# Block-sorted attention feeding a max-of-two MLP: filler matmuls and a new order in the first batch item, and a decaying backlog for choosing the PSUM eviction engine

## The chip, the cores and the metric

The kernel runs on one core of one Trainium2 chip. A core has a matrix engine (TensorE, "PE" in the profile; its weight loads are listed apart as "PEld"), a vector engine (DVE), a scalar engine (ACT), GpSimd (POOL) and a queue engine (SP), each with its own instruction stream. They run side by side and wait for each other on semaphores. TensorE writes its results to PSUM, and only DVE and ACT read them from there here. The metric is device time in microseconds of one execution. Before the change the median of 8 runs was 173.48 us (172.91 to 175.41).

## The reference

```python
# q, k, v: (4, 8, 768, 64); sort_net: (4, 8, 8, 8)
P = sort_net
for _ in range(5):                       # softmax over rows, then columns normalised
    P = np.exp(P - P.max(-1)); P = P / P.sum(-1); P = P / P.sum(-2)
k_sorted = einsum('bhij,bhjcd->bhicd', P, k_b)      # 8 blocks of 96 keys, mixed
v_sorted = einsum('bhij,bhjcd->bhicd', P, v_b)
attn = softmax(scale * q_b @ k_sorted.T)            # inside one block of 96
x = (attn @ v_sorted) -> (3072, 512)
out = np.maximum(x @ w1, x @ w2) @ w_out            # w1, w2: 512x1024, w_out: 1024x512
```

(Shortened: small constants and keepdims are left out.)

## The kernel before

**Algebra.** The kernel uses max(a, b) = relu(a - b) + b. `w_difference` overwrites w1 by w1 - w2 in four column pieces, `moe_h` computes relu(x (w1 - w2)) into a tile `g`, and the part x w2 w_out goes through a product wc = w2 w_out. For it w2 is transposed on TensorE (`w2_transposes`) and multiplied by w_out (`w_product`). `moe_out` sums g w_out and x wc in one PSUM tile.

**Stages of one batch item.** `sort_k` and `sort_v` (or `sort_v_pair` for two items at once) mix the key and value blocks with block-diagonal matrices. `scores(b, u)` computes one of 8 pieces of the scores (four blocks, two heads), and ACT writes its exponential into an `e` tile. `values(b, u)` multiplies `e` with the values; DVE then takes a reciprocal of the row sums (`rs`) and scales the result into `x`. Two pieces of `x` make one `x_transposes` unit (pieces 0 and 1 make unit 0, and so on up to 6 and 7 for unit 3). For item 0 the transposes are done by TensorE with an eviction to `xT`; for later items SP issues DMA transposes. `moe_h(b, ch, t)` reads half of the 768 tokens (`ch`) and a quarter of w1 (`t`).

**Order.** The order is written out by hand and every engine runs its stream in order. Up to line 720 it is a prologue: five Sinkhorn rounds during which TensorE multiplies zeros (`keep_streaming`, line 75), then item 0's sorting, its first scores and values, the first two `moe_h` of item 0, and the transposes of w2. `moe_h_products(0, 0, t, (0, 2))` starts a product with half of its terms as soon as `x_transposes(0, 0)` is evicted; `moe_h(0, 0, t, "A", (1, 3))` adds the rest after `x_transposes(0, 1)`. Then a loop over the four items walks through `units` (8 `moe_h`, for item 0 4 `w_product`, 12 half `moe_out`), puts pieces of the next item's sorting and attention (`steps`) between them in proportion to a `cost` per unit, and `tail` steps at given units. `tail[2]` and `tail[3]` hold what is left of item 0: values 6, x transposes 2, values 7, x transposes 3.

**PSUM.** There are four PSUM buffers of 128 x 1024 floats (line 62), handed out again in the order in which the program releases them. A new TensorE tile therefore waits until the eviction of an older one is done.

**Choice of the eviction engine.** `evac` (line 98) copies a PSUM tile to SBUF on ACT or DVE. Some calls name the engine ("A", "D"); the others, and `moe_h` of later items, call `pick` (line 92). It keeps a sum of estimated nanoseconds per engine in `load` and takes the engine whose sum would be smaller afterwards. The sums grow over the whole kernel and are never reduced.

Of the kernel before, what the change touches and what calls it, by code (L numbers as in the profile page):

```python
# [16 lines left out]
def kernel(  # L17
# [21 lines left out]
    B, H, S, D = q.shape  # L39
# [26 lines left out]
    def ps_f32(name):  # L66
        return psum.tile([128, 1024], FP32, tag="ps", name=name)

    def ps_bf16(name):
        return psum.tile([128, 2048], BF16, tag="ps", name=name)  # L70
# [17 lines left out]


    load = {"A": 0.0, "D": 0.0}  # L90

    def pick(a_ns, d_ns):
        if load["A"] + a_ns <= load["D"] + d_ns:
            load["A"] += a_ns
            return "A"
        load["D"] += d_ns
        return "D"

    def evac(out_ap, in_ap, n, two_x=False, eng=None):
        a_ns, d_ns = (200 + n) / 1.2, (130 + (n / 2 if two_x else n)) / 0.96  # L100
        if eng:
            load[eng] += a_ns if eng == "A" else d_ns
        if (eng or pick(a_ns, d_ns)) == "A":
            nc.scalar.copy(out=out_ap, in_=in_ap)  # L104
        else:
            nc.vector.tensor_copy(out=out_ap, in_=in_ap)  # L106
# [81 lines left out]
    def w_difference(t, eng=None):  # L188
        n = DFF // 4
        (eng or nc.vector).tensor_tensor(  # L190
            out=w1_sb[:, :, t * n : (t + 1) * n],
            in0=w1_sb[:, :, t * n : (t + 1) * n],
            in1=w2_sb[:, :, t * n : (t + 1) * n],
            op=ALU.subtract,
        )
        if not eng:
            load["D"] += 600
# [313 lines left out]
    def x_transposes(b, t, eng=None):  # L511

        ih, hh = divmod(t, 2)
        x = x_tiles.pop((b, ih, hh))
        if b:
            nc.sync.dma_start_transpose(
                out=xT[:, b % 2, ih, hh].rearrange("p h (i c) -> p (h i) c", c=BLK),
                in_=x.rearrange("p t i n d -> p (t i n d)"),
            )
            return  # L520
        ps = ps_bf16("tx_ps")
        for m in range(8):
            h2, ii = divmod(m, 4)
            nc.tensor.matmul(
                ps[:, m * BLK : (m + 1) * BLK],
                x[:, h2, ii].rearrange("p n d -> p (n d)"),
                ident[0:BLK, 0:BLK],
                is_transpose=True,
                start=True,
                stop=True,  # L530
            )

        evac(
            xT[:, b % 2, ih, hh].rearrange("p h f -> p (h f)"),
            ps[:, 0 : 2 * TCH],
            2 * TCH,
            two_x=True,
            eng=eng,
        )
# [5 lines left out]
    def w2_transposes(t, eng):  # L545
        ps = ps_bf16("tw_ps")
        for n in range(16):
            fb, dmt = t * 4 + n // 4, n % 4
            nc.tensor.matmul(  # L549
                ps[:, n * 128 : (n + 1) * 128],  # L550
                w2_sb[:, dmt, fb * 128 : (fb + 1) * 128],
                ident,
                is_transpose=True,
                start=True,
                stop=True,
            )
        return lambda: evac(
            w2T[:, t * 4 : t * 4 + 4, :].rearrange("p f d -> p (f d)"),
            ps,
            2048,  # L560
            two_x=True,
            eng=eng,
        )
# [23 lines left out]
    def moe_h_products(b, ch, t, hps, n=0):  # L587
        if hps[0] == 0:
            h_ps[t] = ps_f32("h_ps")
            keep_streaming(h_ps[t], n)  # L590
        for m in range(2):
            fb = t * 2 + m
            for hp in hps:
                nc.tensor.matmul(  # L594
                    h_ps[t][:, m * 512 : m * 512 + TCH],
                    w1_sb[:, hp, fb * 128 : (fb + 1) * 128],
                    xT[:, b % 2, ch, hp % 2, hp // 2, :],
                    start=(hp == 0),
                    stop=(hp == 3),
                )  # L600

    def moe_h(b, ch, t, eng=None, hps=(0, 2, 1, 3), n=0):
        moe_h_products(b, ch, t, hps, n)
        ps = h_ps[t]
        g = gpool.tile([128, 2, TCH], BF16, tag="g", name="g")
        src = ps.rearrange("p (t f) -> p t f", t=2)[:, :, 0:TCH]
        if (eng or pick((200 + 2 * TCH) / 1.2, (130 + 2 * TCH) / 0.96)) == "A":
            nc.scalar.activation(out=g, in_=src, func=AF.Relu)  # L608
        else:
            nc.vector.tensor_scalar(  # L610
                out=g, in0=src, scalar1=0.0, scalar2=None, op0=ALU.max
            )
        g_tiles[b, ch, t] = g
# [48 lines left out]
    def att(b):  # L662

        SC = [lambda u=u: scores(b, u) for u in range(8)]
        VA = [lambda u=u: values(b, u) for u in range(8)]
        TR = [lambda t=t: x_transposes(b, t) for t in range(4)]
        return SC, VA, TR
# [17 lines left out]
    SC, VA, TR = att(0)  # L685
# [4 lines left out]
    sort_v(0, 1, 0, "A")  # L690
    q_transposes(0, 0, "D")
    sort_v(0, 2, 0, "A")
    SC[0]()
    sort_v(0, 3, 0, "D")
    SC[1]()
    q_transposes(0, 1, "D")
    VA[0]()
    SC[2]()
    VA[1]()
    SC[3]()  # L700
    VA[2]()
    x_transposes(0, 0, "A")
    SC[4]()
    VA[3]()
    moe_h_products(0, 0, 0, (0, 2), 256)
    x_transposes(0, 1, "A")
    SC[5]()
    moe_h_products(0, 0, 1, (0, 2))
    VA[4]()
    w2_out = w2_transposes(0, "D")  # L710
    moe_h(0, 0, 0, "A", (1, 3))
    w2_out()
    w_difference(2)
    SC[6]()
    moe_h(0, 0, 1, "A", (1, 3))
    VA[5]()
    SC[7]()
    w_difference(3)
    for b in range(1, B):
        selections(b)  # L720

# [19 lines left out]
    for b in range(B):  # L741
        units = [lambda t=t: moe_h(b, 0, t, None if b else "A") for t in range(4)]
        if b == 0:
            units[0] = lambda: None
            units[1] = lambda: None
        units += [lambda t=t: moe_h(b, 1, t) for t in range(4)]
        cost = [1.3] * 8
        if b == 0:
            units += [lambda dmt=dmt: w_product(dmt) for dmt in range(4)]
            cost += [1.7] * 4  # L750
        units += [
            lambda ti=ti, part=part: moe_out(b, ti, part)
            for ti in range(6 if b < B - 1 else 4)
            for part in range(2)
        ]
        cost += [1.3] * 12
        if b == B - 1:
            units += [
                lambda: moe_out_last(4, [(0, 512, "D")]),
                lambda: moe_out_last(5, [(0, 384, "D"), (384, 512, "A")]),  # L760
            ]
        steps, lo = [], 2
        if b < B - 1:
            qs = [lambda half=half: q_transposes(b + 1, half) for half in range(2)]
            ks = [lambda t=t, b=b: sort_k(b + 1, t) for t in range(3)]
            SC, VA, TR = att(b + 1)

            def group(*fs):
                return [lambda: [f() for f in fs]]

            if b == 0:
                lo = 8
                vs = [lambda t=t: sort_v(1, t) for t in range(4)]
                for m, c in enumerate((0, 24, 48, 72)):
                    VA[m + 1 : m + 2] = group(VA[m + 1], lambda c=c: turn(both, c))
                steps = group(*ks) + group(*vs[0:2]) + group(vs[2], qs[0]) + group(vs[3], qs[1])
            elif b == 1:
                vs = [lambda t=t: sort_v_pair(2, t) for t in range(8)]
                tail[0] = qs
                tail[10] = [lambda: pair_q(3, 0), lambda: pair_q(3, 1)]  # L780
                steps = group(*ks) + group(*vs[0:2]) + group(*vs[2:4]) + group(*vs[4:6])
                steps += group(*vs[6:8])
            else:
                tail[0] = qs
                lo = 4
                steps = group(*ks)
            steps += group(*SC[0:2]) + VA[0:1] + group(*SC[2:4]) + VA[1:2] + group(VA[2], TR[0])
            steps += group(*SC[4:6]) + VA[3:4] + group(VA[4], TR[1]) + group(*SC[6:8]) + VA[5:6]
            steps += group(VA[6], TR[2]) + VA[7:8] + TR[3:4]
        done = 0  # L790
        for n, unit in enumerate(units):
            unit()
            for step in tail.get(n, []):
                step()
            total = sum(cost[lo:-2])
            want = -(-len(steps) * sum(cost[lo : n + 1]) // total)
            while done < min(want, len(steps)):
                steps[done]()
                done += 1
        tail = {}  # L800
# [28 lines left out]
```

## Time and profile before

| | us |
|---|---|
| median of 8 runs | 173.48 |
| the profiled execution, its own time | 173.4 |
| its span, first to last instruction | 171.5 |
| TensorE busy in the span | 161.8 (94%) |
| DVE busy | 83.3 (49%) |
| ACT busy | 79.9 (47%) |
| GpSimd busy | 27.7 (16%) |
| prologue up to the end of item 0's fourth `moe_h` product | about 33.8 |

The profiled execution took 173.4 us, of which 171.5 us are the span that all rows below are measured in (times in rows are microseconds from the span's start); 1.9 us lie around it. A row of the timeline gives the start, the busy time, the engine, the line of the kernel, the output and input tiles, and how many instructions are merged in it; in square brackets is the idle time of that engine just before, and what ended it. Matmuls overlap each other in the array: one matmul's duration is a latency, and the distance from start to start is what it takes from TensorE.

### The profile page before, as it was taken

How to read it: one execution, taken by the hardware profiler on the slowest of the kernel's cores; microseconds unless marked ns; L12 is line 12 of the kernel's file. 1: busy time of each engine (PE TensorE's matmuls, PEld its weight loads, DVE VectorE, ACT ScalarE, POOL GpSimd, SP SyncE). 2: the span in 40 equal slices, each digit the busy share in tenths (PEclk: the TensorE clock that was granted, in tenths of full speed). 3: DMA queues.
4: the chain of work that ended last, by engine and by line, in shares of the span. 5: the costliest groups of instructions: out<-in, count | busy, mean ns of one | idle time of the engine just before them, and what ended most of it. 6: DMA issues, size and time to landing. Idle time of an engine off the chain costs nothing.

```text
span 171.5 us, 4513 instructions
## 1 busy us (share of the span) xinstructions
PE 161.8 (94%) x1995; PEld 98.7 (58%) x2013; DVE 83.3 (49%) x182; ACT 79.9 (47%) x96; POOL 27.7 (16%) x44
## 2 busy tenths in 40 slices
PE   7999789999899999998999999999899999999992
PEld 7949656755755455556655455557555545654451
DVE  5968766858534687403745735125646410240041
ACT  4577675774656353248774532236632116312000
POOL 7865585231402002000000000000000000000000
PEclk9999999999999999999999999999999999999999
DMA  3999999999999976999200263692022863000333
GB/s 48 206 205 198 200 208 205 219 202 207 219 216 201 205 107 159 148 262 233 66 0 4 46 168 119 109 251 49 0 49 84 133 169 126 0 0 0 122 131 114
DMA packets 30242, 23.09 MB, mean 135 GB/s; under 512 B 16720, under 2 KB 25168, under 8 KB 30224
## 3 DMA queue, kind: packets, MB, share of 16 engines
q0 software_dynamic: 10880, 12.59, 43.5%
q1 hardware_dynamic: 19200, 10.17, 25.1%
q8 instruction: 15, 0.25, 0.6%
q10 hardware_dynamic: 144, 0.07, 0.1%
q14 instruction: 3, 0.02, 0.0%
HBM read 25.17 MB, written 6.29 MB: 183 GB/s over the span
## 4 chain that ended last, share of the span: by engine, by line
PE 88%; DVE 4%; ACT 4%; issue 1%; DVEq 0%; ACTq 0%
PE out_ps L621 36%; PE h_ps L594 25%; PE fill_ps L82 6%; PE wc_ps L572 4%; PE s_ps L459 4%; PE o_ps L486 3%; PE k_ps L392 3%; PE v_ps L413 2%; ACT kT L104 2%; DVE v_sb L106 1%; PE v_ps L434 1%; PE tw_ps L549 1%; DVE qT L106 1%; ACT xT L104 1%; PE tq_ps L367 1%
## 5 line engine op out<-in xcount | busy, mean ns | idle before, releaser
L621 PE MATMUL out_ps<-wo_sb,g 128*128 128x512 bf16 (+2 forms) x188 | 46.1, 370 | 0.8 <-issue 0.3
L594 PE MATMUL h_ps<-xT,w_sb 128*128 128x384 bf16 x256 | 45.0, 326 | 1.2 <-ACT kT L104 0.5
L467 ACT ACTIVATE e<-s_ps 96x768 bf16<-96x768 f32 x32 | 24.3, 803 | 21.3 <-PE s_ps L459 21.3
L594 PEld LDWEIGHTS <-w_sb 128*128 128x128 bf16 x256 | 24.1, 98 | 16.9 <-issue 1.4
L621 PEld LDWEIGHTS <-g 128*128 128x128 bf16 x200 | 17.3, 98 | 16.6
L608 ACT ACTIVATE g<-h_ps 128x768 bf16<-128x768 f32 x22 | 17.8, 811 | 17.5 <-PE h_ps L594 17.4
L621 PE MATMUL out_ps<-wc,xT 128*128 128x512 bf16 (+2 forms) x99 | 24.7, 370 | 0.1
L503 DVE TENSOR_TENSOR x<-o_ps,rs 96x512 bf16<-96x512 f32 x32 | 22.0, 687 | 1.1
L610 DVE TENSOR_SCALAR g<-h_ps 128x768 bf16<-128x768 f32 x10 | 9.6, 958 | 26.0 <-PE h_ps L594 26.0
L104 ACT COPY o<-out_ps 128x1024 f32<-128x1024 f32 x9 | 9.1, 1012 | 26.0 <-PE out_ps L621 20.9
L621 PEld LDWEIGHTS <-xT 128*128 128x128 bf16 x100 | 9.6, 97 | 11.2
L486 PEld LDWEIGHTS <-e 96*128 96x128 bf16 x256 | 11.4, 97 | 6.0 <-ACT e L467 0.4
L497 DVE RECIPROCAL rs<-o_ps 96x8 f32<-96x8 f32 x32 | 6.4, 200 | 16.4 <-PE o_ps L486 16.3
L106 DVE CAST v_sb<-v_ps 96x1024 bf16<-96x1024 f32 x9 | 11.0, 1217 | 5.4 <-PE v_ps L413 4.4
L486 PE MATMUL o_ps<-v_sb,e 96*128 96x65 bf16 x256 | 12.6, 193 | 0.5 <-ACT e L467 0.3
L106 DVE CAST kT<-k_ps 128x1024 bf16<-128x1024 f32 x5 | 6.0, 1222 | 12.0 <-PE k_ps L392 12.0
L459 PE MATMUL s_ps<-qT,kT 64*128 64x96 bf16 x256 | 9.3, 204 | 1.4 <-DVE qT L106 0.9
L459 PEld LDWEIGHTS <-kT 64*128 64x128 bf16 x256 | 6.3, 94 | 6.3 <-issue 5.0
L82 PE MATMUL fill_ps<-fill 128*128 128x138 bf16 x88 | 8.1, 278 | 1.2 <-DVE fill L73 1.2
L82 PEld LDWEIGHTS <-fill 128*128 128x128 bf16 x93 | 8.3, 125 | 1.5 <-DVE fill L73 1.2
L132 POOL DMA_DIRECT2D q_raw<-in_q_dram x7 | 5.5, 804 | 20.0 <-DVE q_pair L341 13.3
L106 DVE COPY o<-out_ps 128x1024 f32<-128x1024 f32 x2 | 2.4, 1224 | 12.4 <-PE out_ps L621 12.4
(75 smaller groups left out, 140.8 us busy)
## 6 DMA issues: line engine op xcount, KB each, us to landing
out_dram<-o SPq DMA_DIRECT2D x11, 512.0 KB, 3.0
k_raw<-in_k_dram POOLq DMA_DIRECT2D x12, 256.0 KB, 12.0
v_raw<-in_v_dram POOLq DMA_DIRECT2D x6, 384.0 KB, 11.7
q_raw<-in_q_dram POOLq DMA_DIRECT2D x3, 768.0 KB, 9.8
w_sb<-in_moe_w_dram POOLq DMA_DIRECT2D x4, 256.0 KB, 9.7
w_sb<-in_moe_w_dram POOLq DMA_DIRECT2D x2, 512.0 KB, 11.2
wo_sb<-in_moe_w_out_dram POOLq DMA_DIRECT2D x2, 512.0 KB, 14.8
v_raw<-in_v_dram POOLq DMA_DIRECT2D x3, 256.0 KB, 5.0
```

The source lines that it names most:

```text
L82: nc.tensor.matmul(ps[:, 0:w], w0, fill[:, 0:w], start=True, stop=True)
L104: nc.scalar.copy(out=out_ap, in_=in_ap)
L106: nc.vector.tensor_copy(out=out_ap, in_=in_ap)
L459: nc.tensor.matmul(ps[:, h2 * 512 + ii * 128 : h2 * 512 + ii * 128 + BLK], kT[b][rows, (hp * 8 + i) * BLK : (hp * 8 + i) * BLK + 128], rhs ...
L467: nc.scalar.activation(out=e[:, 0 : 8 * BLK].rearrange("p (t c r) -> p t c r", t=8, r=R), in_=ps[0:BLK] .rearrange("p (t f) -> p t f", t=8 ...
L486: nc.tensor.matmul(ps[:, h2 * 512 + ii * 65 : h2 * 512 + (ii + 1) * 65], e[:, (h2 * 4 + ii) * BLK : (h2 * 4 + ii) * BLK + 128], v_sb[:, m0 ...
L503: nc.vector.tensor_tensor(out=x, in0=ov[:, :, :, 0:D], in1=rs.to_broadcast([BLK, 2, 4, D]), op=ALU.mult,)
L572: nc.tensor.matmul(wc_ps[0][:, m * 512 : (m + 1) * 512], w2T[:, fb, dmt * 128 : (dmt + 1) * 128], wo_sb[:, fb, :], start=(fb == 0), stop=( ...
L594: nc.tensor.matmul(h_ps[t][:, m * 512 : m * 512 + TCH], w1_sb[:, hp, fb * 128 : (fb + 1) * 128], xT[:, b % 2, ch, hp % 2, hp // 2, :], sta ...
L608: nc.scalar.activation(out=g, in_=src, func=AF.Relu)
L610: nc.vector.tensor_scalar(out=g, in0=src, scalar1=0.0, scalar2=None, op0=ALU.max)
L621: nc.tensor.matmul(dst, g_tiles[b, ch, m // 2][:, m % 2, off : off + 128] if m < NFB else xT[:, b % 2, ch, hp % 2, hp // 2, off : off + 12 ...
```

## The change

It has two parts.

The first is in the prologue. `scores` 0 and 2, `values` 0 and 2 of item 0 get filler matmuls on zeros ahead of their own (1024 or 512 columns, issued as matmuls of 512), and the filler before the first `moe_h_products` grows from 256 to 512 columns. `values` 3 moves ahead of `x_transposes(0, 0)` and `scores` 4; `values` 4 moves ahead of the second `moe_h_products` and `scores` 5; `values` 5 moves ahead of the second `moe_h`. `w2_transposes(0)` and its eviction move from before the first `moe_h` to between `scores` 6 and 7. On DVE `w_difference(2)` and the work of `values` 5 thereby come before the eviction of that transpose.

The second is a function `elapse(ns)` that takes `ns` off both sums in `load`, not below zero. The loop calls it with 1000 times the unit's cost before each unit, and with 250 before each step. The names and numbers that `pick` compares stay as they were. The engine of an eviction changes only from item 2's sorting on: item 2's three `sort_k` go DVE, ACT, DVE (before: ACT, ACT, DVE), several of its `sort_v_pair` and `moe_h` swap engines, the eviction of the first `moe_out` pair of item 1 moves from ACT to DVE and that of item 2 from DVE to ACT, and all of item 3's `moe_h` and its `moe_out` evictions in the loop go to ACT.

```diff
@@ -88,6 +88,10 @@
     load = {"A": 0.0, "D": 0.0}
+
+    def elapse(ns):
+        for e in load:
+            load[e] = max(0.0, load[e] - ns)
 
     def pick(a_ns, d_ns):
@@ -690,32 +694,31 @@
     sort_v(0, 1, 0, "A")
     q_transposes(0, 0, "D")
     sort_v(0, 2, 0, "A")
-    SC[0]()
+    scores(0, 0, 1024)
     sort_v(0, 3, 0, "D")
     SC[1]()
     q_transposes(0, 1, "D")
-    VA[0]()
-    SC[2]()
+    values(0, 0, 512)
+    scores(0, 2, 1024)
     VA[1]()
     SC[3]()
-    VA[2]()
+    values(0, 2, 512)
+    VA[3]()
     x_transposes(0, 0, "A")
     SC[4]()
-    VA[3]()
-    moe_h_products(0, 0, 0, (0, 2), 256)
+    moe_h_products(0, 0, 0, (0, 2), 512)
     x_transposes(0, 1, "A")
+    VA[4]()
+    moe_h_products(0, 0, 1, (0, 2))
     SC[5]()
-    moe_h_products(0, 0, 1, (0, 2))
-    VA[4]()
-    w2_out = w2_transposes(0, "D")
     moe_h(0, 0, 0, "A", (1, 3))
-    w2_out()
     w_difference(2)
+    VA[5]()
+    moe_h(0, 0, 1, "A", (1, 3))
     SC[6]()
-    moe_h(0, 0, 1, "A", (1, 3))
-    VA[5]()
+    w2_transposes(0, "D")()
+    w_difference(3)
     SC[7]()
-    w_difference(3)
     for b in range(1, B):
         selections(b)
 
@@ -789,12 +792,15 @@
         done = 0
         for n, unit in enumerate(units):
+            elapse(1000 * cost[n] if n < len(cost) else 0)
             unit()
             for step in tail.get(n, []):
+                elapse(250)
                 step()
             total = sum(cost[lo:-2])
             want = -(-len(steps) * sum(cost[lo : n + 1]) // total)
             while done < min(want, len(steps)):
+                elapse(250)
                 steps[done]()
                 done += 1
```

## The prediction

> **What bounds the kernel now.** I read the page's busy times and the engine shares of the chain that ended last first, then who TensorE waited for, then the timeline at each of those waits.
>
> ```profile
> PE 161.8 (94%) x1995; PEld 98.7 (58%) x2013; DVE 83.3 (49%) x182; ACT 79.9 (47%) x96; POOL 27.7 (16%) x44
> ...
> PE 88%; DVE 4%; ACT 4%; issue 1%; DVEq 0%; ACTq 0%
> ```
>
> TensorE is the bound: 88% of the chain is its own work, and other engines hold 4% each. Of 171.5 us it is idle 9.7. The profile puts 1.2 before its first matmul, and 3.4 follow its last (168.1 to 171.5). Some 5 us of gaps are left for a change of order to win. Its own waits:
>
> ```profile
> PE s_ps L459 <- DVE qT L106: 0.9, 2, 0.5
> PE h_ps L594 <- ACT kT L104: 0.5, 1, 0.5
> ...
> PE h_ps L594 <- DVE g L610: 0.4, 1, 0.4
> PE tw_ps L549 <- ACT e L467: 0.3, 1, 0.3
> ...
> PE o_ps L486 <- ACT e L467: 0.3, 1, 0.3
> ```
>
> Columns: total us, how often, longest. No wait is over 0.5 us. The first, fourth and fifth lie in the prologue that the first part reorders; the second is where the second part reassigns an eviction; the third stays (below).
>
> **Part 1a: the zeros.** Six more matmuls of 512 zero columns, and one that grows from 256 to 512: 6.5 x 0.24 us = 1.6 us of TensorE time (0.24 from the chain's row of four such fillers, 0.97 us). Each stands where TensorE is idle now. Scores 0 wait from 17.30 to 17.78 for the query eviction (0.48, filler 0.49). Values 0 have 0.24 (19.64 to 19.88) for 0.24. Scores 2 have 0.63 (20.12 to 20.75) for 0.49; values 2 have 0.35 (21.65 to 22.00) for 0.24. So I cost them at 0, from the idle in these rows. If that cover were missing, the price would be the whole 1.6. A gain can come only from a clock that would otherwise fall, so here is the clock. The filler of the Sinkhorn rounds shows what a slow and a fast array look like (columns: share and count of PE, then PEld, PEclk, DMA):
>
> ```profile
> 5.00:6.00 1.00, 1.00 (x12) 1.00 (x9) 1.00 1.09 217
> ...
> 7.00:8.00 1.00, 1.00 (x20) 1.00 (x18) 1.00 1.08 205
> ```
>
> The same 138-column matmul comes 12 times per us at first and 20 times from 7 us on (single durations 322 and 221 ns), while PEclk reads 1.00 throughout. The clock row therefore doesn't show this gate; matmul durations do. In the prologue:
>
> ```profile
> L594 PE MATMUL h_ps<-xT,w_sb x32: 323/326/337, 23.9 to 33.5; 128*128 128x384 bf16 x32
> ```
>
> Minimum, median and maximum of item 0's products from 20 to 35 us are within 4%: always fast. The Trainium skill, *TensorE: Matmul & The Clock Gate*, Part 1, says the gate halves the clock after an idle window of about 3.4 us; the longest wait here is 0.5, so by this rule the zeros win nothing. The same page's section on a second failure mode warns that frequent short idles between PSUM-limited groups can make the clock oscillate too. By that, one 3.4 us window at half speed costs up to 1.7 us, an estimate from the page, and two of the eight executions lie 1.6 and 2.0 us above the profiled one. But the trace shows no such window at 173.4 us, which is the typical execution, so I take 0 and keep a gain of up to 0.5 on the median for the range.
>
> **Part 1b: the new order.** Start-to-start costs by the timeline: scores 0.28, values 0.24, x transposes 0.45, half of a moe_h 0.68, w2 transposes 0.90, whole moe_h 1.41. ACT takes 0.8 for an exponential, an xT eviction or a relu; DVE 0.9 for rs and x. I lay the new order along these, with a handoff of 0.05.
>
> Up to values 2 (22.00) nothing moves. Values 3 then stand directly behind; their exponential is the second of a pair:
>
> ```profile
> 21.14 1.50 ACT L467 ACTIVATE e<-s_ps 96x768 bf16<-96x768 f32 x2 [1.39 <-PE s_ps L459]
> ...
> 23.86 0.81 PE L594 MATMUL h_ps<-xT,w_sb 128*128 128x384 bf16 x4
> ```
>
> It ends at 22.64, so values 3 start at 22.68 and TensorE idles 0.44 from 22.24. Behind it in TensorE's stream are x transposes 0, which before started at 22.46; they now start at 22.92, and ACT ends their eviction at 24.27 instead of 23.81. The first half product starts at 24.32 instead of 23.86: 0.46 late. From there the order gains: values 4 find their exponential (24.98), start at 25.45, and DVE has x 4 at 26.8 (before 27.39). The second half product follows at 25.7, scores 5 at 26.43 (they wait for the xT buffer, 26.38), moe_h 0 ends at 27.4, values 5 wait for exponential 5 until 27.64 (0.25), moe_h 1 ends at 28.56, scores 6, w2 transposes at 28.84 (the 0.3 wait on ACT is gone), scores 7, and moe_h 2 starts at 30.02: exactly where it starts now. The lateness and the gains cancel. Moe_h 3 needs a PSUM buffer from the relu of moe_h 2 and starts at 32.39 (now 32.38).
>
> `w_difference(2)` is now ahead of `rs` 5 on DVE. Its columns land at about 27.6 (GpSimd's query load, which waits for the same transfer, is released at 27.64), so it runs to 28.3 and delays `rs` 5 by 0.2; x 5 at 29.2 is needed at 31.7, so this is hidden. What isn't hidden is the w2 eviction: 1.23 us of DVE that moves from 27.82 to 29.93. Behind it stand `w_difference(3)` (0.68), the selections (0.53), then rs and x of values 6 and 7.
>
> ```profile
> 27.82 1.23 DVE L106 COPY w2T<-tw_ps 128x2048 bf16<-128x2048 bf16 x1 [0.43 <-PE tw_ps L549]
> ...
> 32.84 0.69 DVE L503 TENSOR_TENSOR x<-o_ps,rs 96x512 bf16<-96x512 f32 x1
> ...
> 33.68 0.51 PE L524 MATMUL tx_ps<-ident,x 96*128 96x96 bf16 x8
> ```
>
> Now x 7 ends at 33.53, just ahead of x transposes 3. After: 29.93 + 1.23 + 0.68 + 0.53 = 32.35 with overlaps of 0.02, then two pairs of rs and x of 0.9 each: 34.15. TensorE is ready at 33.80, and x transposes 3 start at 34.20 instead of 33.68: **+0.5 us**, with all of TensorE's later work behind it. Part 1 costs 0.5.
>
> **Part 2: the backlog.** Everything to item 2's sorting (78 us) keeps its engine.
>
> ```profile
> 78.97 1.92 ACT L104 CAST kT<-k_ps 128x1024 bf16<-128x1024 f32 x2
> ...
> 79.91 1.22 DVE L106 CAST kT<-k_ps 128x1024 bf16<-128x1024 f32 x1 [8.57 <-PE k_ps L392]
> ...
> 80.94 1.46 PE L594 MATMUL h_ps<-xT,w_sb 128*128 128x384 bf16 x8 [0.51 <-ACT kT L104]
> ```
>
> ACT is still in a relu until 79.07 and does two evictions in a row to 80.89, while DVE had been idle for 8.57; moe_h 3 needs the second one's buffer. With DVE, ACT, DVE the first starts at 78.75 on DVE, the second runs on ACT from 79.3 to 80.32, and moe_h 3 starts at about 80.4: **-0.5 us**. Following the swapped evictions to 89 by the same durations, I find at most one new wait, of 0.05.
>
> Item 1's first output pair goes to DVE at 97.3 (1.22 for ACT's 1.01). Queued behind it is `rs` 3, 0.96 late; its x then ends at 99.4, and its buffer is next wanted at about 100.5. Price 0. Item 2's pair leaves DVE:
>
> ```profile
> 129.79 1.22 DVE L106 COPY o<-out_ps 128x1024 f32<-128x1024 f32 x1 [2.98 <-PE out_ps L621]
> ...
> 131.90 0.20 PEld L459 LDWEIGHTS <-kT 64*128 64x128 bf16 x8 [0.29 <-DVE x L503]
> ```
>
> That copy delays x 3 to 131.85, and scores 7 wait for x 3's buffer. ACT has been idle since 128.4; with the copy there, x 3 ends at about 130.9 and TensorE goes on: **-0.2 us** (the gap between the two groups of 8 scores, 0.49, less their 0.28). The wait of the third row above, on the relu of moe_h 6 at 121.0, keeps its DVE and its 0.4. Item 3's relus all go to ACT: 0.81 each against 1.30 or more of TensorE work per moe_h, so none is late; the last two copies and the end are untouched.
>
> **Sum.** 173.4 (the profiled execution; the median of 173.48 is the same time) + 0.5 - 0.5 - 0.2 = **173.2 us**. Less than 1% (1.7 us) either way is about what a measurement of this kernel can't tell from no change.
>
> **The rivals.**
> 1. *The zeros keep the clock*, 173.2 less 0.5 and more: 172.5. For it: two of eight executions of before at 175.0 and 175.4, about the price of one slow window, and TensorE only half busy in stretches of the prologue. Against: every duration above is a fast one, and these two executions don't set a median. 0.15.
> 2. *Slower: x transposes 3 wait, and part 2 gives nothing back.* The mechanism is that DVE's queue behind the late w2 eviction ends after TensorE's moe_h 3. It decides from the moment that x 7 ends later than about 33.85. Its price is 0.5 as laid out, plus 0.2 if the fillers end later than the waits that they cover (0.01 to 0.02 each by the rows, up to 0.1 where a filler's buffer comes late). The gains of part 2 vanish if the new kT order brings the wait one step further, to the values' eviction on ACT behind the relu: 173.4 + 0.7 = 174.1. For it: the DVE count; against: the gain at 78 us has TensorE as the only follower, and I find no second wait. 0.25, of which 0.08 lies over 175.1, with the fillers wholly unhidden (+1.6) on top of the wait.
> 3. *The new order wins where I see a draw*: if the exponential that values 3 wait for came as early as the first of its pair (21.95), the 0.44 falls away and the prologue ends 0.4 sooner before x 7; but x 7 is what ends last there, so only what moves DVE forward counts. 172.8 at best. 0.08.
> 4. *It does nothing*: the engines chosen by `pick` don't matter and the prologue's end is set by x 7 as before: 173.4. 0.07.
>
> My case has 0.45. The range: low 172.2 takes in rivals 1 and 3 and leaves some 0.08 below; high 174.5 takes in rival 2's centre with half a microsecond, and leaves some 0.10 above. Faster by over 1% (under 171.7) would need two thirds of a slow window on the median: 0.07. Slower by over 1% (over 175.2): 0.09. Within: 0.84.
>
> **What the profile after would show.** Item 0's values 3 start near 22.7 with a wait on ACT's exponential before them; the first half product starts at about 24.3; the w2 eviction starts near 29.9; moe_h 2 starts at 30.0. X transposes 3 wait for DVE's x and start near 34.2. The filler's 512-column matmuls last 379 ns and no 384-column one more than about 340. Between 78 and 82 the wait on ACT kT is gone, and the distance from k's first matmul to moe_h 3 falls from 2.85 to 2.3. Near 131 the wait on DVE's x is gone. I am wrong if TensorE's matmuls in the prologue of either kernel are seen at the slow rate, if a new wait over 0.3 us stands between 80 and 135, or if moe_h 2 starts 0.5 or more away from 30.0.

## The result and the profile after

The changed kernel takes 172.67 us (median of 20 runs, 172.44 to 173.32) against 173.29 us before (57 runs, 172.81 to 175.72). The ratio is 0.9961, with a 95% interval of 0.9946 to 0.9976: faster by 0.4%, clear of noise and below 1%. The forecast was 173.2. (The ratio leaves out executions over 1.5% above their kernel's fastest.) The two lowest times differ by 0.37 us, the medians by 0.62. That difference is half of the story below.

The profiled execution of after took 172.67 us with a span of 170.8. First its busy times and the chain that ended last:

```profile
PE 161.9 (95%) x1999; PEld 97.5 (57%) x2019; DVE 78.3 (46%) x177; ACT 84.6 (50%) x101; POOL 27.7 (16%) x44
...
PE 82%; DVE 10%; ACT 3%; issue 2%; DMA 1%; DVEq 0%
```

TensorE is still the bound. DVE holds 10% of the chain instead of 4% because the chain now begins with the Sinkhorn steps on DVE, where in the profile of before it began with the start filler on TensorE. This is not the change: in this execution the array reached its fast rate sooner (20 filler matmuls per us from 5 us on, where before still had 12 between 5 and 6), so the filler ended before the Sinkhorn result was there. Item 0's first query transpose starts at 15.31 instead of 15.70, a gift of 0.39. The same place lies between 15.11 and 15.78 in the profiles of the other kernels below, but for the one with 80 start fillers, whatever parts of the change they have. I therefore measure the rest from that transpose (before, then after):

```profile
15.70 0.23 PE L360 MATMUL tq_ps<-ident,fill 128*128 128x128 bf16 x1
```

```profile
15.31 0.23 PE L364 MATMUL tq_ps<-ident,fill 128*128 128x128 bf16 x1
```

Whom TensorE waited for, longest first:

```profile
PE h_ps L598 <- DVE g L614: 0.4, 1, 0.4
PE s_ps L463 <- DVE qT L110: 0.4, 2, 0.2
...
PE h_ps L598 <- ACT xT L108: 0.3, 1, 0.3
PE o_ps L490 <- ACT e L471: 0.3, 1, 0.3
```

(Line numbers of after are 4 higher.) The wait on ACT kT is gone and that on qT is halved, as fillers now stand in it. A wait on ACT xT is new. Item 0 in the timeline:

```profile
22.30 0.42 PE L490 MATMUL o_ps<-v_sb,e 96*128 96x65 bf16 x8 [0.28 <-ACT e L471]
...
23.94 0.81 PE L598 MATMUL h_ps<-xT,w_sb 128*128 128x384 bf16 x4 [0.29 <-ACT xT L108]
...
29.60 1.22 DVE L110 COPY w2T<-tw_ps 128x2048 bf16<-128x2048 bf16 x1 [0.83 <-PE tw_ps L553]
...
32.94 0.69 DVE L507 TENSOR_TENSOR x<-o_ps,rs 96x512 bf16<-96x512 f32 x1
...
33.68 0.37 PEld L528 LDWEIGHTS <-x 96*128 96x128 bf16 x8 [0.46 <-DVE x L507]
```

Values 3 wait for their exponential, the first half product comes late, the w2 eviction is late on DVE, x 7 ends at 33.63, and x transposes 3 wait for it. From the first query transpose to x transposes 3 it is 17.98 before (15.70 to 33.68) and 18.38 after (15.31 to 33.69): **+0.40**. Then item 2's keys:

```profile
78.11 1.71 PE L396 MATMUL k_ps<-bd,k_raw 64*64 64x64 bf16 x96
...
78.91 2.36 DVE L110 CAST kT<-k_ps 128x1024 bf16<-128x1024 f32 x2 [7.56 <-PE k_ps L396]
...
79.34 1.01 ACT L108 CAST kT<-k_ps 128x1024 bf16<-128x1024 f32 x1 [0.26 <-PE k_ps L396]
...
80.53 1.48 PE L598 MATMUL h_ps<-xT,w_sb 128*128 128x384 bf16 x8
```

From k's first matmul (78.11) to moe_h 3 it is 2.42 instead of 2.85 (78.09 to 80.94): **-0.43**. And item 2's first output pair:

```profile
129.34 1.01 ACT L108 COPY o<-out_ps 128x1024 f32<-128x1024 f32 x1 [1.30 <-PE out_ps L625]
...
131.02 0.51 PE L463 MATMUL s_ps<-qT,kT 64*128 64x96 bf16 x16
...
131.47 0.60 PE L625 MATMUL out_ps<-wo_sb,g 128*128 128x512 bf16 x2
```

The same place before:

```profile
131.42 0.83 PE L459 MATMUL s_ps<-qT,kT 64*128 64x96 bf16 x16
...
132.18 0.61 PE L621 MATMUL out_ps<-wo_sb,g 128*128 128x512 bf16 x2
```

The 16 score matmuls run through; before they stood in two groups with a wait between. The first output matmul after them starts at 131.47, 0.45 behind the first score, where before it was 0.76 (131.42 to 132.18): **-0.31**. The three add up to -0.34 us, and with the 0.39 at the start to the 0.7 between the spans.

### The profile page after: what moved, and what is told of

Its sections match the earlier page's. It is cut to its first block, busy times and chain, and to the rows that moved or that the text cites. A ratio compares the mean times of both kernels' runs of the same rounds, so it can differ in the third digit from the quotient of the medians.

```text
span 170.8 us, 4524 instructions
## 1 busy us (share of the span) xinstructions
PE 161.9 (95%) x1999; PEld 97.5 (57%) x2019; DVE 78.3 (46%) x177; ACT 84.6 (50%) x101; POOL 27.7 (16%) x44
## 4 chain that ended last, share of the span: by engine, by line
PE 82%; DVE 10%; ACT 3%; issue 2%; DMA 1%; DVEq 0%
PE out_ps L625 36%; PE h_ps L598 23%; PE wc_ps L576 4%; PE o_ps L490 4%; PE s_ps L463 4%; PE k_ps L396 3%; PE v_ps L417 2%; PE v_ps L438 1%; DVE v_sb L110 1%; ACT e L471 1%; ACT kT L108 1%; PE tw_ps L553 1%; DVE qT L110 1%; DMA p_sb<-in_sort_net_dram 1%; PE tq_ps L371 1%
## 5 line engine op out<-in xcount | busy, mean ns | idle before, releaser
L612 ACT ACTIVATE g<-h_ps 128x768 bf16<-128x768 f32 x27 | 21.9, 811 | 14.1 <-PE h_ps L598 14.1
L108 ACT COPY o<-out_ps 128x1024 f32<-128x1024 f32 x10 | 10.1, 1012 | 29.9 <-PE out_ps L625 25.2
L110 DVE CAST kT<-k_ps 128x1024 bf16<-128x1024 f32 x6 | 7.2, 1221 | 20.2 <-PE k_ps L396 20.2
L660 DVE COPY o<-out_ps 128x512 f32<-128x512 f32 (+1 forms) x2 | 1.2, 625 | 28.9 <-PE out_ps L625 28.9
L82 PEld LDWEIGHTS <-fill 128*128 128x128 bf16 x99 | 7.6, 113 | 1.8 <-DVE fill L73 1.2
L82 PE MATMUL fill_ps<-fill 128*128 128x138 bf16 x88 | 7.0, 254 | 1.2 <-DVE fill L73 1.2
L149 POOL DMA_DIRECT2D k_raw<-in_k_dram x12 | 6.5, 544 | 8.2 <-DMA wo_sb<-in_moe_w_out_dram 4.6
```

What stands on the lines that cost most here:

```text
L82: nc.tensor.matmul(ps[:, 0:w], w0, fill[:, 0:w], start=True, stop=True)
L149: nc.gpsimd.dma_start(out=k_raw[b][:, ci * n : (ci + 1) * n], in_=k_src[b, :, ci * n : (ci + 1) * n],)
```

## The experiments

The theory from the traces (1): three shifts, +0.4, -0.4 and -0.3, and the zeros cost nothing. The rival (2): the zeros hold the array's clock in the prologue, in executions that the one trace of before doesn't show. The kernels were measured in three series, each on one chip together with the kernel before; a comparison of kernels from two series is the weaker one.

**Zeros alone.**

```diff
-    SC[0]()
+    scores(0, 0, 1024)
...
-    VA[0]()
-    SC[2]()
+    values(0, 0, 512)
+    scores(0, 2, 1024)
...
-    VA[2]()
+    values(0, 2, 512)
...
-    moe_h_products(0, 0, 0, (0, 2), 256)
+    moe_h_products(0, 0, 0, (0, 2), 512)
```

> Before, with only the five filler edits of the prologue. Theory 1 (waits and order explain the result): the zeros lie in idle time, so the lowest time stays at 172.8 and the median within 0.2 of 173.3; values above 174 stay as frequent as before (9 of 57). Theory 2 (the zeros keep the array fast in the prologue's lulls): the lowest time stays, the median falls by 0.3 or more, and times above 174 disappear.

Measured: 173.21 median, 173.06 to 173.57 in 6 runs, ratio 0.9991 (0.997 to 1.0011). Before, in the same series: 173.47, 172.94 to 176.31 in 11. The lowest time rises by 0.1, and from the first query transpose to x transposes 3 the trace has 18.07 (15.29 to 33.36) against 17.98: the zeros cost 0.1 at most, so nearly all of them lie in idle time. Nothing is above 174, as (2) expects, but the median falls by 0.26 only, and six runs are few.

**Order alone.**

```diff
+    VA[3]()
     x_transposes(0, 0, "A")
     SC[4]()
-    VA[3]()
...
-    SC[5]()
+    VA[4]()
     moe_h_products(0, 0, 1, (0, 2))
-    VA[4]()
-    w2_out = w2_transposes(0, "D")
+    SC[5]()
     moe_h(0, 0, 0, "A", (1, 3))
-    w2_out()
     w_difference(2)
+    VA[5]()
+    moe_h(0, 0, 1, "A", (1, 3))
     SC[6]()
-    moe_h(0, 0, 1, "A", (1, 3))
-    VA[5]()
+    w2_transposes(0, "D")()
+    w_difference(3)
     SC[7]()
-    w_difference(3)
```

> Before, with only the prologue's new order: no new zeros and no decaying backlog. Theory 1: plus 0.4 on the lowest time (173.2), because x transposes 3 wait for the late w2 eviction on DVE; times above 174 are as frequent as before. Theory 2: the new order has shorter lulls too, so the long times may become rarer, but the lowest time still rises by 0.4.

Measured: 174.54 median, 173.33 to 175.98 in 6 runs, ratio 1.004 (1.0005 to 1.0074). The lowest time is 0.4 above that of before in the same series, as both expect. But four of the six have a mean clock of 0.99 or 0.98 and take 174.46 and more. Its profiled execution is one of them, so the slow stretch can be seen. Shares by us of the span (PE, PEld, DVE, ACT, POOL with their counts, then PEclk, DMA, GB/s):

```profile
21.00:22.00 1.00, 0.69 (x16) 0.42 (x16) 0.92 (x3) 1.00 (x2) 0.80 (x1) 1.00 1.25 203
22.00:23.00 1.00, 0.76 (x19) 0.68 (x21) 0.96 (x3) 0.19 (x1) 0.70 (x1) 0.97 1.26 208
23.00:24.00 1.00, 0.87 (x11) 0.45 (x11) 0.73 (x2) 0.96 (x2) 1.00 (x1) 0.50 1.23 205
24.00:25.00 1.00, 1.00 (x4) 0.45 (x3) 0.00 (x0) 0.54 (x1) 1.00 (x3) 0.50 1.29 222
25.00:26.00 1.00, 1.00 (x15) 0.88 (x12) 0.00 (x0) 0.00 (x0) 1.00 (x3) 0.50 1.19 195
26.00:27.00 1.00, 1.00 (x12) 0.55 (x9) 0.52 (x2) 0.80 (x1) 1.00 (x3) 0.83 1.25 205
```

The granted clock is exactly half from about 22.94 (0.97 of that us) to 26.34 (0.83), that is for 3.4 us. Inside it the first half product takes 1.44 instead of 0.81:

```profile
23.89 1.44 PE L594 MATMUL h_ps<-xT,w_sb 128*128 128x384 bf16 x4
```

Just ahead of it lies this stretch of 3.4 us, in the kernel with the new order alone:

```profile
19.50:22.90 3.40, 2.38 (x56) 1.81 (x55) 3.25 (x8) 1.50 (x2) 2.71 (x2) 1.00 1.32 205
```

and in the changed kernel, with the zeros:

```profile
19.50:22.90 3.40, 2.87 (x59) 2.11 (x58) 3.25 (x7) 1.50 (x2) 2.87 (x2) 1.00 1.31 205
```

TensorE is busy for 2.38 of 3.4 us without the zeros and 2.87 with them. No single wait there is over half a microsecond: the clock fell after many short ones. A second trace with a slow stretch, that of values 3 alone (below), has it from about 22.3 to 25.7 by the same reckoning, again 3.4 us, with TensorE busy for 2.19 of the 3.4 us ahead of it.

A low busy share alone doesn't bring the fall. The profiled execution of the change without its zeros (below) has the same order and the same share in the same stretch, and its clock reads 1.00 there and behind it:

```profile
19.50:22.90 3.40, 2.38 (x56) 1.86 (x55) 3.25 (x7) 1.50 (x2) 2.86 (x2) 1.00 1.31 205
```

The kernel before has 2.42 there in its trace, and its clock stays too. What decides in which execution it falls stays open.

**Backlog alone.** The second part of the change without the first:

```diff
+    def elapse(ns):
+        for e in load:
+            load[e] = max(0.0, load[e] - ns)
...
+            elapse(1000 * cost[n] if n < len(cost) else 0)
             unit()
...
+                elapse(250)
                 step()
...
+                elapse(250)
                 steps[done]()
```

> Before, with only the decaying backlog. Theory 1: minus 0.7 on the lowest time (172.1) and on the median (172.6): 0.4 at the wait on ACT kT near 80 and 0.3 at the wait on DVE's x near 131. Theory 2: the same on the lowest time, but the long times stay (some over 173.5), since the prologue is that of before.

Measured: 172.25 median, 172.09 to 173.03 in 6 runs, ratio 0.9937 (0.9915 to 0.9959). This is what both expected of the lowest time (172.1). One run of the six, the 173.03, has a mean clock of 0.99. By its median and its lowest time the second part alone is faster than the whole change (172.67, 172.44), though from another series, and the two ratio intervals just touch.

**Selections later**, on top of the change:

```diff
-    for b in range(1, B):
-        selections(b)
...
-        2: [VA[6], TR[2], VA[7]],
+        2: [VA[6], TR[2], VA[7], lambda: [selections(b) for b in range(1, B)]],
```

> The changed kernel with the selections for items 1 to 3 (0.53 us of DVE) moved from before to behind values 7. Theory 1: x 7 comes 0.5 earlier, x transposes 3 no longer wait, minus 0.4: lowest 172.0, median 172.3. If instead something else ends last there (the w2 eviction or a PSUM buffer), it stays at 172.7.

Measured: 172.47 median, 172.36 to 172.9 in 6 runs. That is 0.2 under the change, half of what was expected (from another series; the trace says the same). In its trace the wait on DVE's x is gone, and from the first query transpose to x transposes 3 it is about 0.25 shorter. The other 0.15 of the new order's cost isn't DVE's queue: moe_h 2 starts 14.46 behind the first query transpose in the change and 14.32 before.

**Zeros and backlog, old order.** The edits of the first and the third experiment together:

> Before, with the zeros and the decaying backlog but the old order of the prologue. The new order costs 0.4 in the trace and the zeros keep the clock: lowest 172.2, median 172.3, nothing over 173.0, so 0.4 less than the changed kernel. If the new order pays where the zeros are present, it is at 172.7 or above.

Measured: 172.30 median, 172.15 to 172.91 in 12 runs, ratio 0.9948 (0.993 to 0.9966). Against the change it is 0.4 less on the median and 0.3 on the lowest time; the two ratio intervals overlap, but the traces agree: from the first query transpose to x transposes 3 it is 17.98 here (15.73 to 33.71), as before, and 18.38 in the change. So the order's cost is real also beside the zeros. No run has a mean clock under 0.996.

**The change without its zeros.**

```diff
-    scores(0, 0, 1024)
+    SC[0]()
...
-    values(0, 0, 512)
-    scores(0, 2, 1024)
+    VA[0]()
+    SC[2]()
...
-    values(0, 2, 512)
+    VA[2]()
...
-    moe_h_products(0, 0, 0, (0, 2), 512)
+    moe_h_products(0, 0, 0, (0, 2), 256)
```

> The changed kernel with its new zeros taken out (256 columns before the first half product, as before). If the zeros hold the clock in the new order: lowest 172.5, but about half of the executions 1 us and more above it with a mean clock of 0.99 or less, median 173.5 or more. If the slow stretch seen with the new order alone was a rare accident: median 172.6, as with the zeros.

Measured: 173.66 median, 172.56 to 174.21 in 12 runs, ratio 1.0003 (0.998 to 1.0026). Five have a mean clock of 0.99. The lowest time is 0.1 above that of the change, the median 1.0. By these medians the change without its zeros is no gain. The slow stretch isn't all of it: the seven executions with a mean clock of 0.998 or more have a median of 173.09, still 0.4 above the change. One of them, at 174.1, has a span of only 171.2, so part of its time lies outside the span; for the others the reason is open. Its profiled execution, with the full clock, has moe_h 2 at 14.48 behind the first query transpose (15.30 to 29.78), as the change has with the zeros (14.46).

**Values 3 alone moved.**

```diff
     VA[2]()
+    VA[3]()
     x_transposes(0, 0, "A")
     SC[4]()
-    VA[3]()
```

> Before, with values 3 alone moved ahead of x transposes 0 and scores 4. The trace of before gives x transposes 0 and the first half product 0.46 later, while x 7 stays last before x transposes 3: between 0 and plus 0.5 on the lowest time (172.8 to 173.3). The second wait for an exponential in a row lowers TensorE's share in that stretch: if this is what lets the clock fall, executions with a mean clock of 0.99 become more frequent than before's (9 of 57 over 174).

Measured: 173.93 median, 173.21 to 175.93 in 12 runs, ratio 1.0023 (0.9988 to 1.0058). The lowest time is 0.3 above before's in the same series (172.88). Four of 12 have a mean clock of 0.991 or less; before has 9 of 30 there in the same series. So this one move doesn't make the clock fall visibly more often; 12 executions couldn't show a small rise.

**The executions counted.** Over these series and the measurement of the change, I count the executions whose mean clock is on record (for before, the 54 of the series; the 57 of the result have none) and is 0.992 or less. Half the clock for 3.4 of 171 us gives a mean of 0.990.

| | executions | with a mean clock of 0.992 or less |
|---|---|---|
| before | 54 | 19 |
| order, backlog or values 3 alone, change without zeros | 36 | 14 |
| all seven kernels with the new zeros | 66 | 0 |

The seven kernels are the change, zeros alone, selections later, zeros and backlog, and the three starts with zeros. This settles (2) as far as the mean clock goes: a third of before's executions have the mean of a slow stretch, and none of the 66 with the zeros. Where it lies is seen in two traces only, of kernels other than before. In before the 19 have a median of 173.92 and the other 35 of 173.21, so 0.7 between them. Three of the 19 take 175.2 to 175.75 at 0.990 to 0.992, more than one such stretch explains; that stays open.

**The start.** Executions of one kernel with a full clock still differ by half a microsecond. The profiled one of zeros and backlog (172.65, where the lowest is 172.15) suggests why, in its chain of waits (start, us, what):

```profile
9.40 2.54 PE fill_ps L82 x11
...
11.94 0.16 PE pe L303 x2
```

Its start filler ran at 12 matmuls per us until 7 us, and the selection matmul stood behind the filler until 11.94; the profile after the change has it at 11.46, released by DVE. So I shortened the filler, from zeros and backlog:

```diff
-    keep_streaming(ps_f32("fill_ps"), 88 * 138, most=138)
+    keep_streaming(ps_f32("fill_ps"), 80 * 138, most=138)
```

> As the kernel with zeros and backlog in the old order, and the filler at the start cut from 88 to 80 matmuls of 138 columns (0.5 us of TensorE at the fast rate). If the executions half a microsecond above the lowest time come from a start filler that is still running at the slow rate when the Sinkhorn result is there: the lowest time stays at 172.2 and none lies over 172.5. If that spread has another cause, it stays as it is; and if the filler is then too short to hold the clock, times over 173 appear.

Measured: 174.38 median, 174.09 to 175.11 in 7 runs, ratio 1.0068 (1.0041 to 1.0094): slower, for a reason that none of the three named. The selection matmul is at 11.36, but TensorE then stops at places where the profile shows nothing that it waits for:

```profile
15.83 0.26 PE L417 MATMUL v_ps<-bd,v_dc 64*128 64x64 bf16 x3 [0.64 <-issue]
...
22.02 0.24 PE L490 MATMUL o_ps<-v_sb,e 96*128 96x65 bf16 x2 [0.32 <-issue]
```

Each is inside a row of like matmuls, and a third of 0.49 is at 49.2. To tell a shorter filler from a shorter stream of instructions, I took about the same work out by narrower matmuls (1056 columns against 1104), and in another kernel four matmuls instead of eight:

```diff
-    keep_streaming(ps_f32("fill_ps"), 88 * 138, most=138)
+    keep_streaming(ps_f32("fill_ps"), 88 * 126, most=126)
```

> As the kernel with zeros and backlog in the old order, with the start filler still 88 matmuls but 126 columns wide instead of 138: the same work taken out as by cutting 8 of them, with the number of TensorE instructions unchanged. If the stops without a visible wait in the shorter-start kernel come from the changed number of instructions, they are gone here: lowest 172.2, median 172.3, and none over 172.6, because the start filler ends sooner also when it runs at the slow rate. If they come from the shorter filler itself, this kernel lies at 174 too.

```diff
-    keep_streaming(ps_f32("fill_ps"), 88 * 138, most=138)
+    keep_streaming(ps_f32("fill_ps"), 84 * 138, most=138)
```

> As the kernel with zeros and backlog in the old order, with 84 start fillers instead of 88: 8 TensorE instructions (weights and matmul) fewer instead of 16. If the place of the instructions in the stream matters, the stops may come with less, more or nothing of the 1.9 us seen with 80; if a shorter filler costs by itself, about half: lowest 173.1. If neither, lowest 172.2.

Measured, in this order: 172.27 (172.06 to 172.37, 8 runs, ratio 0.9911, 0.9881 to 0.9941) and 172.16 (172.13 to 172.43, 6 runs, ratio 0.9914, 0.9881 to 0.9947). This fits a start filler that had outlasted the Sinkhorn result: both are 0.4 or more below the change, and the spread is 0.3 instead of 0.8 with 88 fillers of 138 columns. The stops don't come from the shorter filler as such. That they hang on how many instructions stand before a given one fits, but 84 has fewer too and no stops. Why 80 has them stays open.

## Why the prediction was right, and where it was not

**The sum.** +0.5, -0.5 and -0.2 were forecast and +0.40, -0.43 and -0.31 are in the traces; -0.2 against -0.34, and -0.37 between the lowest times. The three places are those that the prediction named. The median of 172.67 is nevertheless 0.5 under the forecast of 173.2 and nearer to rival 1's 172.5, which had a chance of 0.15: it lies in the range because the range had been widened for that rival. (The chances of 0.08 below, 0.84 within and 0.10 above the range add up to 1.02.)

- *X transposes 3 behind DVE's queue*: shown in part. There are 0.46 of wait on DVE's x and 0.40 on the path; with the selections later the wait is gone and 0.25 of the 0.40 with it. The other 0.15 is the lateness of moe_h 2, next point, which the prediction had at 0. The term is 0.1 too large: from the start of the w2 eviction to `rs` 6 it is 2.29 (29.60 to 31.89), where I summed 2.42. I took overlaps of 0.02 from instruction to instruction, and in these rows they are 0.06 to 0.09 (the w2 eviction ends at 30.82, the next starts at 30.75).
- *Values 3*: it starts at 22.30, 6.99 behind the first query transpose, as worked out (22.68 - 15.70 = 6.98), and the first half product comes 0.47 late for 0.46. The lateness doesn't cancel fully by moe_h 2: 0.14 is left.
- *Item 2's keys*: 0.43 for 0.5. The first eviction starts on DVE at 78.91, not 78.75: I took the end of its product too early. The 32 values matmuls behind take 0.85 instead of 0.70, which fits a wait for that buffer.
- *Item 2's output pair*: 0.31 for 0.2. I put 0.28 for each group of 8 scores; the 16 run through in 0.45, and with 0.56 for them the sum would give 0.2.
- *Item 1's pair on DVE at 0, item 3's relus on ACT at 0, the wait on the relu of moe_h 6 unchanged*: all as said.

**The step that failed** is the gain of the zeros, put at 0. Their cost of 0 was right to within 0.1. Their gain was not: the prediction said that the trace shows no slow window at 173.4 us, "which is the typical execution, so I take 0", and gave the clock 0.15 as rival 1. In 19 of 54 executions of before the mean clock is that of a slow window, and with the zeros in 0 of 66. That moves the median too: it fell by 0.62, of which the lowest times explain 0.37; the other 0.25 fits the 0.26 that the zeros alone took off the median in six runs. One profiled execution and eight times couldn't give that share. Two of eight at +1.6 and +2.0 were a hint that I set aside, though their clocks aren't on record and one window (about 1.1) is less than they lost. "The clock row therefore doesn't show this gate" was also wrong: it reads 1.00 while the start filler runs at the slow rate, and 0.50 in a window that begins later.

**The two rules of the clock page.** The idle-window rule of the Trainium skill, *TensorE: Matmul & The Clock Gate*, Part 1, on which I took 0, doesn't describe this case: no wait was over 0.5 us, and the clock fell. Its section on a second failure mode, short idles between PSUM-limited groups, comes nearer: the waits ahead of the fall were short ones for evictions on DVE and ACT. The estimate of 1.7 us for a window is an upper end. In the run with the new order alone moe_h 2 starts 15.58 behind the first query transpose (15.25 to 30.83), and 14.48 in the same order at full clock: 1.1 us.

**Rival 2** (slower) needed part 2 to give nothing back; its two places gave 0.74 in the traces. What the prologue's new order brings by itself is a loss of 0.3 to 0.4.

## What to carry to other kernels

Where TensorE is idle in many short waits, ask the mean clock of several executions, not one trace. Here a third of the executions had a slow window by that measure; with zeros that fit into the waits none had, at a cost of 0.1 us at most. An engine chooser that sums work over the whole kernel forgets that an idle engine has caught up; letting the sums fall with time was worth 0.7 us in the traces here. After moving a step, follow the queue of the engine that evicts it: the order cost 0.4, of which 0.25 because a DVE copy came 2 us later, and dropping that order makes the kernel faster than the change, 172.2 with a shorter start filler.

## What the runs showed that I had not expected

- The clock fell to exactly one half for 3.4 us behind a stretch in which TensorE was busy for 2.38 of 3.4 us and never idle for more than 0.5 us at once. In another execution the same share brought no fall.
- The granted clock reads 1.00 in the first microseconds while the same 138-column matmul lasts 322 ns, and when it later lasts 221 ns.
- When the fast rate begins differs from execution to execution (5 us in the profile after the change, 7 us in that of zeros and backlog). In the later one the selection matmul stood behind the start filler until 11.94 instead of 11.46: 0.5 us.
- Eight start fillers fewer made TensorE stop for 0.64, 0.32 and 0.49 us with nothing to wait for, at places up to 49 us on; four fewer didn't. Its cause wasn't settled.
